# An S5 and an H3 layer in one kernel: the same operations under another written-out order

## The chip, the core and the metric

The kernel runs on one NeuronCore of a Trainium2 chip. The metric is the device time of one execution in microseconds. PE is TensorE, DVE is VectorE, ACT is ScalarE, POOL is GpSimd and SP is SyncE; SP does no arithmetic here and only issues DMAs.

## What is computed

Two sequence layers over 2048 tokens and 640 channels, their outputs side by side in one 2048 x 1280 result.

```python
# A (S5): a complex diagonal recurrence between two projections
Lam_bar = exp(dt * Lam);  B_bar = ((Lam_bar - 1) / Lam)[:, None] * Bmat
Bu = einsum("bld,pd->blp", x, B_bar)
for t in range(L):
    h = Lam_bar * h + Bu[:, t]            # hs collects h
y = 2 * einsum("blp,dp->bld", hs, Cmat).real + x * Dskip
# B (H3): a four-tap shift convolution, then a long convolution over the sequence
k_shift = sum(k_pad[:, t:t + S] * shift_k[:, ks - 1 - t] for t in range(4))
kv = k_shift * v
y = irfft(rfft(kv, 2 S) * rfft(ssm_k, 2 S))[:S] + kv * ssm_D
out_B = q * y
```

## The kernel before

**A program and an order.** `build` lists 779 operations, each with the engines that may run it, the stretch of memory that it reads and writes, and, where it uses PSUM, a group that takes one or two of PSUM's eight banks. `depend` derives from the footprints which operation must follow which. `emit` then walks through `ORDER`, a string with one word for each operation, and issues them in that order; each engine works through its own words strictly in turn. A word is the operation's number, the engine that runs it and its first bank:

```python
order = [(int(x[:-2]), x[-2].upper(), int(x[-1])) for x in ORDER.split()] ...
c.P.narrow = {int(x[:-2]) for x in ORDER.split() if x[-2] == "t"}
```

A stands for ACT, V for DVE, G for POOL, T or t for PE (t: a first Fourier step in its narrow form), S for SP. An operation that opens a group waits until the last one that held its banks is done:

```python
if o is o.group.ops[0]:
    need |= {held[b] for b in own if held[b] is not None}
```

All tiles lie in one SBUF tile, `arena`, at fixed places, and PSUM is one tile, `acc`; so the profile names nearly every operand `arena` or `acc`, and lines tell the operations apart.

**Part A.** `load_x` brings x in eight transposed pieces (x0 to x7), `load_B` the input matrix (two parts by a transposing DMA, B2, the rest by way of PE, `turn_B`). The recurrence is a tree over 16 neighbouring steps. `up2` (ten of them, L558; pieces x4 to x7), `up1` (five, L558 and L579; x2 and x3) and `up0a` to `up0c` (x0 and x1) multiply by B and combine pairs of steps with the matrices RR; `coarse` scans over the blocks of 16 (`cs_...`, mostly DVE); `down` spreads the result over the steps again. A `down` sum is added by DVE (L701), or, where ACT evicts it (L699), PE first adds the old value through an identity matmul (L681) for each matmul of its own (L682). `project` is C0 to C15, each 20 matmuls (L718): it loads 128 rows of x (`ld_r`, L709), multiplies them by Dskip (`xd`, L710), adds them to the product (`ev_C`, L720) and stores (`st_A`, L724). Four row buffers turn over, so a load waits for the store four uses before it.

**Tables.** On POOL: integer phases, by `iota` (w_m, g_m: L289, L327) and products (w_q L291, g_q L330, phs L449, phc L452), which wait in part for parameters that a chain of small DVE operations works out; fn1 (L386) is the first on POOL that needs them. ACT makes sines of them (w_s, g_s L334, sin, cos, al_s). DVE makes the RR from them (al, then `rr`, L436).

**Part B.** `load_kv` brings k and v by transposing DMAs (k into a single buffer); `conv` works out kv: four multiplications (`cm`, L199 on ACT, L198 on DVE), three sums (`ca`, L799; the product of each tap goes through one scratch buffer) and the product with v (`cx`, L800). `plane` (`pl`, L806) stores kv to `kv_rows` in HBM and `relay` (`rl`, L816) loads it in another layout. The Fourier transforms are matmuls: `s1` (L835, narrow L840; evicted by `e1`, L845) and `s2` (L859; `e2`, L872) for the filter (h) and for kv (k), in two halves of channels; `product` multiplies the spectra (pp, pq, py, pz: L883 to L890); `r2` (L904; `er2`, L909) and `r1` (L925) go back; `er1` multiplies by q (L937) and `store` writes (`st_B`, L949). `addD` (L768) adds ssm_D to the filter; the first `s1h0` operations need addD0.

**Around the change.** In the first 62 us PE runs up2, up1, up0a and the filter's s1h0 between them; DVE and ACT evict all of them and run conv, POOL builds tables, SP issues the loads one behind the other. Evictions are named `ev_` and the operation.

Of the kernel before, what the change touches and what calls it, by code (L numbers as in the profile page):

```python
# [1040 lines left out]
def plain_order(P):  # L1041
# [16 lines left out]


ORDER = (  # L1060
# [38 lines left out]
)  # L1099


# [68 lines left out]
```

## Time and profile before

| | |
|---|---|
| median of 3 runs (lowest to highest) | 199.89 us (198.49 to 203.23) |
| profiled execution, its own time | 199.76 us |
| its span | 197.9 us |
| mean granted clock of PE | 0.975 |
| instructions | 7928 |
| HBM read / written | 11.32 MB / 7.86 MB |

A row of a timeline is: start and length in us, engine, line and operation, result<-inputs, shapes, and in brackets the idle time of the engine before it with what ended it. A piece of the chain is: start, length, what. A row of the stage view is: the stretch, its length, then busy us (and instructions) of PE, PE's weight loads, DVE, ACT and POOL, the granted clock, the busy share of the DMA engines and GB/s. A row of a group is: line, engine, operation, shapes and count, then busy us, mean ns of one, idle us before them.

### The profile page before, as it was taken

The page shows a single profiled execution, that of the slowest core. Times are in us where ns is not written, and L with a number is a line of the kernel's source. Part 1 is how long each engine was busy: PE and PEld are TensorE (multiplying, and loading weights), DVE is VectorE, ACT ScalarE, POOL GpSimd, SP SyncE. Part 2 cuts the span into 40 slices and gives each one's busy share as a digit, 9 for nine tenths or more (in the row PEclk, how much of TensorE's full clock was granted, in tenths as well). Part 3 has the DMA queues.
Part 4 walks back from the last instruction along what each step waited for, and adds up shares of the span by engine and source line. Part 5 has one row for each costly group of instructions (what it writes and reads, how often), then busy time and mean ns, then how long its engine had stood idle before and what let it go on. Part 6 is the DMA issues. An engine that isn't in the chain of part 4 may idle for free.

```text
span 197.9 us, 7928 instructions
## 1 busy us (share of the span) xinstructions
PE 178.1 (90%) x3546; PEld 119.9 (61%) x3549; DVE 173.3 (88%) x230; ACT 134.0 (68%) x160; POOL 76.5 (39%) x63
## 2 busy tenths in 40 slices
PE   5699999779999999788978999999999999999970
PEld 1386555345567765556656666567677867887750
DVE  3969998999789899999999999999999999858650
ACT  2076999845998798999969799796377640870000
POOL 6869972940020400341704465840220604605000
PEclk9799999969999999999999999999999999999996
DMA  6999999599599999899993899002599805433995
GB/s 140 224 206 160 170 170 146 125 183 176 121 231 213 174 179 124 134 193 137 149 251 80 223 165 192 8 3 68 114 211 213 168 14 155 111 85 83 233 208 160
DMA packets 106685, 30.19 MB, mean 153 GB/s; under 512 B 101275, under 2 KB 106011, under 8 KB 106651
## 3 DMA queue, kind: packets, MB, share of 16 engines
q1 hardware_dynamic: 106158, 29.18, 81.0%
q8 instruction: 28, 0.46, 1.1%
q10 hardware_dynamic: 492, 0.50, 1.0%
q14 instruction: 7, 0.05, 0.1%
HBM read 11.32 MB, written 7.86 MB: 97 GB/s over the span
## 4 chain that ended last, share of the span: by engine, by line
PE 41%; DVE 20%; POOL 16%; DMA 9%; issue 7%; ACT 5%; DVEq 0%; ACTq 0%; POOLq 0%
PE acc L718 17%; PE acc L558 8%; POOL arena L291 5%; POOL arena L799 4%; PE acc L904 4%; ACT arena L872 4%; PE acc L859 3%; DMA arena<-in_B_ssm_D_dram 3%; PE acc L840 3%; POOL arena L330 3%; PE acc L925 2%; DMA kv_rows<-arena 2%; DMA arena<-in_A_Lambda_re_dram 2%; DVE arena L872 2%; DVE arena L198 2%
## 5 line engine op out<-in xcount | busy, mean ns | idle before, releaser
L558 PE MATMUL acc<-arena 128*64 128x512 bf16 (+1 forms) x440 | 46.8, 369 | 0.1
L718 PE MATMUL acc<-arena 128*128 128x320 bf16 x320 | 45.7, 300 | 0.6 <-DVE arena L720 0.4
L872 ACT CAST arena<-acc 128x960 bf16<-128x960 f32 (+1 forms) x38 | 33.3, 910 | 9.2 <-PE acc L859 7.4
L718 PEld LDWEIGHTS <-arena 128*128 128x128 bf16 x320 | 30.4, 98 | 13.3 <-DVE arena L720 1.0
L558 PEld LDWEIGHTS <-arena 128*64 128x64 bf16 x440 | 24.6, 113 | 18.7 <-issue 2.4
L845 ACT CAST arena<-acc 128x1024 bf16<-128x1024 f32 x32 | 31.1, 1024 | 7.0 <-PE acc L840 6.6
L909 ACT CAST arena<-acc 128x1024 bf16<-128x1024 f32 x18 | 17.4, 1026 | 9.9 <-PE acc L904 9.8
L859 PE MATMUL acc<-arena 128*64 128x160 bf16 x512 | 21.8, 235 | 1.4 <-ACT arena L845 0.4
L859 PEld LDWEIGHTS <-arena 128*64 128x64 bf16 x512 | 18.1, 110 | 6.4 <-ACT arena L872 1.7
L710 POOL TENSOR_TENSOR arena<-arena 128x640 bf16<-128x640 bf16 x9 | 12.3, 1399 | 15.9 <-DVE arena L888 9.3
L799 DVE TENSOR_TENSOR arena<-arena 128x2048 bf16<-128x2048 bf16 x13 | 18.2, 1401 | 0.3
L720 DVE TENSOR_TENSOR arena<-acc,arena 128x640 bf16<-128x640 f32 x16 | 13.1, 823 | 5.8 <-PE acc L718 4.8
L799 POOL TENSOR_TENSOR arena<-arena 128x2048 bf16<-128x2048 bf16 x2 | 8.3, 4154 | 22.5 <-DVE arena L198 22.5
L886 POOL TENSOR_TENSOR arena<-arena 128x1280 bf16<-128x1280 bf16 x4 | 10.6, 2656 | 16.2 <-DVE arena L883 10.7
L701 DVE TENSOR_TENSOR arena<-acc,arena 128x1024 bf16<-128x1024 f32 (+1 forms) x14 | 16.1, 1169 | 0.3 <-PE acc L682 0.2
L888 POOL TENSOR_TENSOR arena<-arena 128x1280 bf16<-128x1280 bf16 x3 | 8.3, 2772 | 20.0 <-DVE arena L886 19.9
L840 PE MATMUL acc<-arena 64*64 64x64 bf16 x960 | 11.8, 195 | 4.4 <-POOL arena L330 2.5
L840 PEld LDWEIGHTS <-arena 64*64 64x64 bf16 x960 | 9.6, 108 | 9.9 <-issue 4.1
L937 DVE TENSOR_TENSOR arena<-acc,arena 128x960 bf16<-128x960 f32 (+1 forms) x12 | 12.1, 1041 | 2.1 <-PE acc L925 2.1
L198 DVE TENSOR_SCALAR arena<-arena 128x2048 bf16<-128x2048 bf16 (+2 forms) x19 | 12.6, 674 | 1.1 <-issue 0.5
L682 PE MATMUL acc<-arena 128*128 128x512 bf16 (+2 forms) x50 | 12.3, 328 | 0.5 <-ACT arena L845 0.5
L883 DVE TENSOR_TENSOR arena<-arena 128x2560 bf16<-128x2560 bf16 x8 | 12.0, 1504 | 0.2
(142 smaller groups left out, 289.3 us busy)
## 6 DMA issues: line engine op xcount, KB each, us to landing
out_dram<-arena SPq DMA_DIRECT2D x32, 160.0 KB, 3.5
arena<-in_B_ssm_k_dram SPq DMA_DIRECT2D x8, 320.0 KB, 6.4
kv_rows<-arena SPq DMA_DIRECT2D x5, 512.0 KB, 3.5
arena<-kv_rows SPq DMA_DIRECT2D x16, 160.0 KB, 4.4
arena<-in_A_x_dram SPq DMA_DIRECT2D x16, 160.0 KB, 3.6
arena<-in_B_q_dram SPq DMA_DIRECT2D x8, 320.0 KB, 5.7
arena<-in_A_B_im_dram ACTq DMA_DIRECT2D x2, 160.0 KB, 4.1
arena<-in_A_B_re_dram ACTq DMA_DIRECT2D x1, 160.0 KB
```

The lines of the kernel that those rows point to most:

```text
L198: vm = lambda e: lambda out, in_, by: e.tensor_scalar_mul(out=out, in0=in_, scalar1=by)
L558: e.matmul(o[64 * r:64 * r + 64], lhsT=self.BT[j][:, r, d, :], rhs=self.XP[:, d, lo:lo + n], start=(d == 0), stop=(d == 4), skip_group_che ...
L682: e.matmul(B[:, o], lhsT=c.RR[:, n, j, :], rhs=fr(j, q, k), start=not by_pe, stop=True, skip_group_check=True)
L701: e.tensor_tensor(out=o, in0=b, in1=o, op=ALU.add)
L718: e.matmul(B[:, 512 * b:512 * b + 320], lhsT=lh[j], rhs=self.CT[:, j, 320 * b:320 * b + 320], start=(j == 0), stop=(j == 9))
L720: P.add(f"ev_C{i}", {PDVE: dve(640)}, lambda e, B: e.tensor_tensor(out=ys.rearrange("p (b n) -> p b n", b=2), in0=B.rearrange("p (b n) -> ...
L799: P.add(f"ca{d}_{j}", tt, lambda e: e.tensor_tensor(out=t1, in0=t1, in1=t2, op=ALU.add), outs=[t1], ins=[t1, t2])
L840: e.matmul(B[64 * b:64 * b + 64, 512 * l + 64 * i:512 * l + 64 * i + 64], lhsT=lh[i][ps], rhs=F[ps, b, 64 * l:64 * l + 64], start=True, st ...
L845: P.add(f"e1{what}{hf}_{u}", {PACT: act(1024), PDVE: dve(1024)}, lambda e, B: c.CP[e](out=out, in_=(B.rearrange("p (l n s k) -> p k s l n" ...
L859: e.matmul(B[64 * s:64 * s + 64, 512 * b + 160 * i:512 * b + 160 * i + 160], lhsT=c.W[:, k, 64 * b:64 * b + 64], rhs=self.AS[hf][:, k, 160 ...
L872: c.CP[e](out=out, in_=b.rearrange("p r (k j n) -> p r k j n", k=n, j=4) if nj > 1 else b.rearrange("p r (k x) -> p r k x", k=n))
L909: P.add(f"er2{hf}_{u}", {PACT: act(1024), PDVE: dve(1024)}, lambda e, B: c.CP[e](out=out, in_=B.rearrange("p (s n b) -> p b s n", s=2, n=4 ...
```

## The change

`ORDER` alone is replaced. It has the same 779 words' numbers; 53 of them name another engine or queue: 38 evictions, convolution taps and small copies change between DVE and ACT (19 each way), seven go from DVE to POOL (xd0, xd1, xd7, xd10, xd12, py0, pz1) and five from POOL to DVE (k0, one pq0, xd4, one py1, xd11), and three small loads change between ACT and SP. Among the `down` sums, ad0_2 and ad1_6 go to ACT and ad0_9 to DVE. The narrow forms are the same ones. Banks differ in many places. The head and the tail of the string:

```diff
 ORDER = (
-    "152A0 50G0 140S0 109V0 0V0 75V0 145G0 98G0 6T0 26G0 141G0 153A0 77S0 38G0 146S0 147A0 41G0 168S0 78A0 22G0 13G0 8G0 14V0 "
-    "59G0 4T1 76A0 159S0 15V0 19V0 7G0 18V0 57V0 9V0 112V0 16V0 23V0 111V0 58V0 17V0 28V0 3T0 60G0 148T1 35V0 24V0 167S0 71G0 "
...
-    "698S0 680V4 771T0 686S0 687S0 685S0 697S0 688S0 761T4 772V0 767V2 760V0 768S0 696S0 773S0 762V4 763S0"
+    "146A0 26G0 152S0 0V0 41G0 75V0 5T0 76A0 77S0 98G0 7G0 147A0 167S0 135G0 50G0 71G0 153A0 6T1 78S0 8G0 59G0 158S0 9V0 99G0 "
+    "67G0 1T0 13G0 15V0 16V0 14V0 19V0 17V0 18V0 51V0 168S0 53V0 150T1 57V0 33V0 58V0 28V0 68G0 80T0 4T2 81V0 82A0 140S0 156T0 "
...
+    "771T2 767V4 768S0 770G0 698S0 696S0 695S0 760G0 761T4 697S0 772V2 688S0 687S0 773S0 778S0 762V4 763S0"
 )
```

The stretches that matter, read engine by engine (names for numbers, the bank behind a colon):

```text
PE, up2 to the first s1h0
- up21_0 21_2 21_2 21_0 21_4 21_6 21_8  up20_2 20_0 20_8 20_4 20_6  up1_0:6 up1_4:2 s1h0_0:6 s1h0_7:0 up1_8:4 ...
+ up21_0 21_2 21_0 21_4 21_8 21_6 21_2  up20_8 20_0 20_6 20_4 20_2:4  up1_0:0 s1h0_1:4 s1h0_7:2 up1_4:6 up1_6:2 ...
POOL, from the first operation that needs parameters to the table gm
- fn1 off fn fn fn s16 ph g_m phs w_q w_q w_m w_m g_q w_q phc addD0 w_q g_q g_q r16 gm      (one g_q ahead of fn1)
+ fn1 w_m g_m w_q sw phs fn fn c30 fn g_q g_q dm0 ph w_q w_m w_m w_q w_q g_q addD0 phc r16 gm (one g_q ahead of fn1)
DVE, ahead of the first s1h0
- ev_up21_0 f1 rr rr na ev_up20_2 ca0_2 cm0_1 ca0_1 ma rr cm0_0 rr ev_up20_6 ev_up1_0 ca0_0 e1h0_7
+ cm0_2 ev_up21_4 ca0_2 ev_up21_6 ev_up20_8 al f1 rr rr ca0_1 cm0_0 ev_up20_6 ev_up20_2 ev_up1_0 e1h0_7 ca0_0 rr
ACT, the same stretch
- f1_s al_s ev_up21_2 cm0_3 i_s ev_up21_6 g_s cm0_2 g_s ev_up21_4 w_s w_s ev_up20_0 ev_up20_8 ...
+ ev_up21_0 cm0_3 ev_up21_8 f1_s cm0_1 g_s g_s al_s i_s ev_up21_2 w_s ev_up20_0 sin ev_up20_4 ...
SP, the first loads
- ld_sk par Braw0 x7 B2 x6 B2 k0 x4 x5 x3 h0 h0 x2 h0 h0 D v0 k1 v1 x0 D x1 C0 k2 C0 pl0 v2 pl1 ...
+ Braw1 par x6 par B2 x7 sk B2 k0 x4 x5 h0 h0 x2 h0 x3 D h0 v0 k1 C0 v1 x0 x1 pl0 Dr k2 v2 C0 pl1 ...
DVE, from cs_v0 to cx4 (some left out)
- e2h0_12 e2h0_30 cs_v0_m cx2 cs_a0 cm3_2 cs_w0 cs_s0 ... cx3 ev_gC3_0 ev_gC0_0 cm4_3 cm4_2 e2k0_0 ... addD1 pp0 xd0 ev_C0 e1h1_6 e2k0_8 cx4
+ e2h0_9 cx2 cs_v0_m cs_a0 cs_w0 cs_s0 cm3_3 ... cx3 cm4_3 cm4_2 ad1_0 e2k0_0 ... addD1 pp0 ev_C0 e1h1_6 e2k0_8 e1h1_2 cx4
SP, the stores and loads around cx4
- v4 r1 r3 pl3 rl1 pl4 q1 st_A0 rl1 ...
+ v4 st_A0 rl1 pl3 pl4 rl1 ...
SP, the tail
- st_A10 r9 r11 r8 r14 st_B0 st_A11 r15 st_A9 r13 st_B0 st_A8 5x st_B0 st_A15 r12 st_B1 st_B0 st_B1 st_B1 st_B1 st_B1 st_B1 st_B1 st_A13 st_B1 st_A14 st_A12
+ r11 st_B0 st_A11 r15 st_A9 st_A8 st_B0 st_B0 st_A10 st_B0 r13 4x st_B0 r14 st_B1 r12 st_B1 st_A13 6x st_B1 st_A14 st_A15 st_A12
PE, the tail (both)
  C8, three r11, C15, three r11 (their order differs), C13, C14, C12
```

70 rows, old and new, of the table ORDER are left out of this document.

## The prediction

> **What bounds the kernel now.** The page comes first: its busy line, its slices and the chain that ended last.
>
> ```profile
> PE 178.1 (90%) x3546; PEld 119.9 (61%) x3549; DVE 173.3 (88%) x230; ACT 134.0 (68%) x160; POOL 76.5 (39%) x63
> PE   5699999779999999788978999999999999999970
> PEclk9799999969999999999999999999999999999996
> PE 41%; DVE 20%; POOL 16%; DMA 9%; issue 7%; ACT 5%; DVEq 0%; ACTq 0%; POOLq 0%
> ```
>
> The reader is to see an engine that is hardly ever free: PE is busy 178.1 of 197.9 us and holds 41% of the chain, and DVE is nearly as full. An order can win only where PE's digit is below 9: in the first three slices, in slices 8 and 9 (35 to 45 us), in some of 17 to 22, and in the tail. The chain of waits in order of time names those places.
>
> ```profile
> 40.78 0.76 PE acc L840 x64
> 41.54 3.86 PE acc L558 x20
> ...
> 59.35 2.28 PE acc L558 x20
> 61.63 0.46 PE acc L579 x8
> ...
> 108.07 4.51 DMA kv_rows<-arena
> ...
> 191.93 0.82 DVE arena L720
> ```
>
> The same twenty matmuls of L558 take 3.86 us at 41.54 and 2.28 us at 59.35. The stage view and the timeline of PE show why.
>
> ```profile
> 40.00:50.00 10.00, 9.22 (x214) 4.99 (x216) 9.82 (x12) 5.59 (x5) 2.02 (x2) 0.83 0.89 171
> 90.00:100.00 10.00, 9.55 (x168) 6.50 (x159) 9.49 (x12) 9.97 (x14) 4.06 (x1) 1.00 1.20 135
> 130.00:140.00 10.00, 9.96 (x196) 7.17 (x182) 9.52 (x11) 7.74 (x9) 1.11 (x1) 1.00 0.12 37
> ```
> ```profile
> 10.98 7.22 PE L558 MATMUL acc<-arena 128*64 128x256 bf16 x102
> 40.78 0.41 PE L840 MATMUL acc<-arena 64*64 64x64 bf16 x27 [2.51 <-POOL arena L330]
> ```
>
> PE idles 2.51 us ahead of 40.78, and in 40 to 50 us the granted clock is 0.83 where the other two stages have 1.00. One stall, paid twice: 2.51 idle and 3.86 - 2.28 = 1.6 at a slow clock, 4.1 us in all. From 120 us on PE works through (9.96 of 10.00 in 130 to 140), so the order cannot win there.
>
> The profile puts that idle down to a POOL product of L330. I read it otherwise: the waiting instruction is the first of s1h0_0, whose result goes to bank 6, and bank 6 is freed by ev_up1_0 on DVE, whose row below ends at 40.68.
>
> ```profile
> 18.34 3.17 DVE L436 TENSOR_TENSOR arena<-arena 128x1280 bf16<-128x1280 bf16 x1
> 21.43 3.18 DVE L436 TENSOR_TENSOR arena<-arena 128x1280 bf16<-128x1280 bf16 x1
> 31.64 1.22 DVE L799 TENSOR_TENSOR arena<-arena 128x2048 bf16<-128x2048 bf16 x1
> 32.86 1.48 DVE L436 TENSOR_TENSOR arena<-arena 128x1280 bf16<-128x1280 bf16 x1
> 39.47 1.21 DVE L599 CAST arena<-acc 128x1024 bf16<-128x1024 f32 x1
> ```
> ```profile
> 11.43 0.19 POOL L386 COPY arena<-arena 128x10 int32<-128x10 int32 x1 [1.71 <-DVE arena L378]
> 16.23 3.93 POOL L291 TENSOR_TENSOR arena<-arena 128x1024 int32<-128x1024 int32 x2
> 23.22 3.14 POOL L291 TENSOR_TENSOR arena<-arena 128x1024 int32<-128x1024 int32 x1
> 33.58 1.20 POOL L768 TENSOR_TENSOR arena<-arena 128x80 bf16<-128x80 bf16 x1 [4.94 <-DMA arena<-in_B_ssm_D_dram]
> ```
>
> DVE is late because it takes turns with POOL. The spread rr (L436) lasts 1.48 us at 32.86, when POOL rests, and 3.17 at 18.34, when POOL is in the two products of 16.23 that end at 20.16: 20.16 + 1.4 is its end. In return the product of 23.22 takes 3.14 instead of 3.93 / 2 = 1.96, for DVE's second rr runs until 24.61. So an operation of DVE with both inputs in the arena and a product of POOL exclude each other.
>
> **The change part by part.** No instruction is added or removed but one: two of the `down` sums (ad0_2, ad1_6) go from DVE to ACT and one (ad0_9) comes back. The rest is order, banks, 53 operations on other engines or queues, and the queue of SP.
>
> **1. The first stage, to the end of up0a_0 (before: 61.63 + 0.46 = 62.1).** POOL's products are packed differently: after fn1 (11.43, which I leave there, since the chain of small DVE operations ahead of it is as long) come all four w_q and three g_q, phs and ph, and only then addD0; phc follows. Unblocked that is 7 x 1.96, 2.3 for phs and some 4 of small ones, 20 us: 31.8. ACT decides when DVE can go on:
>
> ```profile
> 17.19 2.00 ACT L199 ACTIVATE arena<-arena 128x2048 bf16<-128x2048 bf16 x1 [1.40 <-DMA arena<-in_B_k_dram]
> 21.09 1.15 ACT L334 ACTIVATE arena<-arena 128x1024 bf16<-128x1024 int32 x1
> ```
>
> cm0_3 ends at 19.2 again (same load of k); ca0_2 on DVE must let a g_q finish and ends near 22; ACT's cm0_1 writes the buffer that ca0_2 reads, 22 to 24; two g_s of 1.15 follow, then al_s at 26.2. From there DVE and POOL alternate: al, f1 to 27.0; rr 1.4; w_q 1.85; rr 1.4; w_q 1.85; ca0_1 1.15; g_q 1.85; cm0_0 0.75: 37.2. addD0 ends at 38.4, and DVE's next two, ev_up20_6 and ev_up20_2 (1.21 each, as the row of 39.47), at 39.5. On PE, s1h0_1 stands right behind up1_0 and writes bank 4, which ev_up20_2 frees. PE begins up2 at about 11.3 (10.98 before; x7 is issued after x6 and half of B2), needs 2.28 x 24 / 20 = 2.7 for an up1, and for the ten up2 what it needed before (it ran from 10.98 to 40.78 - 2.51 with ten up2 and two up1, so 27.3 - 5.4 = 21.9): up1_0 ends at 35.9. So it waits some 3.6 us, the old stall moved forward, with one up1 less done ahead of it.
>
> Then, to the end of up0a_0: before 62.1 - 40.8 = 21.3 with 1.6 of slow clock in it; after 39.5 + 19.7 + 2.7 for up1_4 = 61.9 at full clock, 63.5 if the clock drops. Against 62.1 that is -0.2 or +1.4; without knowing which, **+0.6**. The ends: no wait at all gives 35.9 + 22.4 = 58.3, -3.8; +4.1 on top is rival B. Cover: PE is fed to 35.9 by up2 and up1_0, and nothing hides the rest.
>
> [...]
>
> **2. From up0c to pl4 (62 to 112).** DVE sets the pace (9.49 of 10.00 in 90 to 100, and the chain runs through it to pl4's transfer at 108.07). Its rows by kind:
>
> ```profile
> L845 DVE CAST arena<-acc 128x1024 bf16<-128x1024 f32 x8 | 9.7, 1220 | 1.4 <-PE acc L840 1.4
> L710 DVE TENSOR_TENSOR arena<-arena 128x640 bf16<-128x640 bf16 x7 | 3.4, 482 | 0.0
> L552 DVE CAST arena<-acc 128x640 bf16<-128x640 f32 x3 | 2.4, 809 | 0.0
> L681 PE MATMUL acc<-arena 128*128 128x512 bf16 x8 | 3.1, 383 | 0.1
> ```
>
> Between cs_v0_m and cx4 DVE loses ev_gC0_0 (0.81, now ACT), cx2 (1.22, as the row of L799; now ahead of cs_v0_m, where DVE waits for PE anyway) and xd0 (0.48, now on POOL, which was free there), and gains e1h1_2 (1.22, ahead of cx4). PE does 0.4 more of s2h0 ahead of cs_v0. Sum -0.81 - 1.22 - 0.48 + 1.22 + 0.4 = **-0.9**. If ACT (9.97 of 10.00 in 90 to 100) is late with ev_gC0_0, 0.8 of it goes. The wait added on SP, st_A0 for ev_C0 ahead of pl3 and pl4, holds pl3 back to about 105; pl4 cannot go before cx4 anyway, so it costs 0 to 0.6, and I take 0.
>
> **3. 112 to the last C.** PE's own work decides. ACT evictions of `down` make PE add the old value through an identity: two more by ACT, one fewer, each of two 512-wide matmuls at some 0.22 start to start (L681's 383 ns overlap): 2 x 0.22 = **+0.4**. The moves of pq0, py0, py1, pz1 between DVE and POOL have slack: r20 and r21 are behind a C of 2.8 us each.
>
> **4. The tail.**
>
> ```profile
> 179.25 0.33 SPq L724 DMA_DIRECT2D out_dram<-arena  x1
> ...
> 185.88 5.73 SPq L949 DMA_DIRECT2D out_dram<-arena  x8
> ...
> 193.52 1.53 SPq L724 DMA_DIRECT2D out_dram<-arena  x2
> ```
>
> From st_A8 (179.25) to the last store SP issues 20 DMAs almost without a pause, to 195.05; its last two go out from 193.52, when ev_C12 has been done since 192.75 (191.93 + 0.82), so SP itself is late there. In the new queue 24 stand at st_A8 or behind it: ld_r13, ld_r14, st_A10 and one st_B0 more. At the cheapest price, 0.33, four cost 1.3; at the mean of 15.8 / 20 = 0.79 they cost 3.2; under waits, nothing. I take **+0.7**. It also brings ld_r12 closer to xd12 and ev_C12; by the rows that still just fits.
>
> **The sum.** The profiled execution lasted 199.76: 197.9 of span and 1.9 around it. 199.76 + 0.6 - 0.9 + 0.4 + 0.7 = 200.6. The median shown, 199.89, is 0.1 above that execution, so nothing is shifted.
>
> **The rivals.**
> **A, the early stall goes.** If POOL and DVE collide less than I chain them, PE runs on at 35.9: -3.8, and no slow clock. Half of the gain of part 2 is lost with it, DVE being the next bound: 199.76 - 3.8 - 0.5 + 0.4 + 0.7 = 196.6. For it: DVE has one rr and one ev less ahead of the critical eviction. Against: every two-input row beside POOL took the long time.
> **B, slower: x1 arrives late.** SP puts half of C0 (3.99 us of issue) ahead of v1, x0 and x1, and k1 must wait for cm0_0.
>
> ```profile
> 43.35 3.99 SPq L533 DMA_TRANSPOSE arena<-in_A_C_im_dram  x1
> ```
> ```profile
> arena<-in_A_x_dram SPq DMA_TRANSPOSE x8, 5.3
> ```
>
> k1 goes out at 37.3 (behind cm0_0, 37.2); k1 and v1 at 2 each, C0 at 4 and the two x at 1.5 each end their issue at 48.3; x1 lands 5.3 later, 53.6, and up0a_4 comes on PE at 53 to 54.7. It decides as soon as x1 is over 2.5 us behind PE: 2.5 of idle and 1.6 of clock, 200.6 + 4.1 = 204.7. For it: DMA is near full there (0.89). Against: no landing of that stage held PE before.
> **C, nothing moves.** The bound after 120 us is PE's work, the same but for 0.4, and early gains or losses are taken up by DVE: 199.76 + 0.4 = 200.2.
> **D, SP in the tail.** The four issues at 0.79, 3.2 instead of 0.7: 200.6 + 2.5 = 203.1.
>
> **How the numbers follow.** Forecast 0.38, A 0.20, B 0.10, C 0.20, D 0.12. A measurement here tells about 2% (4 us) from no change. Range 196.6 to 203.6: A's point, and D with part of B; it leaves out A's lower half and most of B. Over 2% faster (below 195.9) needs A with part 2 whole: 0.13. Over 2% slower (above 203.9): B and a little of D, 0.12. Within: 0.75. Predicted time 200.6.
>
> **What would show it.** Part 1: PE idle ahead of s1h0_1 between 36 and 39.5 and rr at 2.5 us or more; no idle there, or granted clock 1.00 in 30 to 50, speaks for A. B: PE waiting at L558 for in_A_x. Part 2: kv_rows' last store about 0.4 us sooner than 108.07. Part 3: twelve instead of eight 512-wide identity matmuls. Part 4: SP without a pause from st_A8 on, and more than the 6.0 us of before from the end of C12 (191.9) to the end of the span (197.9). My chain in part 1 would be wrong if POOL's and DVE's operations did not alternate one by one.

## The result and the profile after

The changed kernel is slower: median 207.1 us of four executions (204.66 to 209.35) against 199.38 of the kernel before on the same chip, ratio 1.0365 (95%: 1.0265 to 1.0465). The profiled execution took 204.66, with a span of 202.9. The median is understood only with the spread: of ten executions, these four and six more below, three took 204.6 and seven 207.1 to 209.7, and the ratio leaves the slowest out.

The page of the changed kernel, its busy line, slices and chain:

```profile
PE 179.4 (88%) x3548; PEld 121.0 (60%) x3551; DVE 170.6 (84%) x228; ACT 131.0 (65%) x160; POOL 79.2 (39%) x65
PE   5399979899999989889979999999899799899850
PEclk9769999999999999999999999999999999999995
DMA  6999999799999999799977999460786102206986
PE 43%; DVE 23%; POOL 11%; DMA 7%; SPq 5%; issue 5%; ACT 1%; POOLq 1%; DVEq 0%
```

PE is busy 1.3 us longer than before and stands 3.7 longer. The low clock of slices 8 and 9 is gone; instead the low stretch in the head, slices 2 and 3, has grown from 3.4 to 6.8 us. In slices 32 to 36 the DMA engines rest at zero to two tenths, right ahead of the stores at the end, and SP's own queue holds 5% of the chain. The waits of PE, by what ended them (line, releaser, us in total, times, longest):

```profile
PE acc L356 <- DMA arena<-in_A_log_dt_dram: 2.5, 1, 2.5
...
PE acc L904 <- DVE arena L872: 1.2, 1, 1.2
PE acc L558 <- DVE arena L575: 1.0, 1, 1.0
...
PE acc L840 <- POOL arena L452: 1.0, 1, 1.0
...
PE acc L718 <- DVE arena L720: 0.9, 1, 0.9
```

These are new: the head (log_dt's load), r20_8 at 159.6 (L904), up20_0 at 28.0 (L558), s1h0_1 at 40.6 (L840) and C12 at 192.6 (L718). Operation by operation, after against before:

| ends at, us | before | after |
|---|---|---|
| begin of the first up2 | 10.98 | 13.43 |
| up0a_0 | 62.07 | 62.89 |
| cs_s0 | 72.69 | 72.62 |
| cs_h1 | 87.34 | 89.35 |
| cx4 | 108.04 | 109.58 |
| C7 | 154.25 | 154.55 |
| C8 | 178.26 | 180.84 |
| C12 | 191.89 | 195.51 |
| span | 197.9 | 202.9 |

Of the 1.5 us at cx4 only 0.3 are left at C7. Then 2.3 are lost between C7 and C8, 1.0 more up to C12, and 1.4 behind it. (Some 0.6 is only moved from ahead of C7 to behind it, with r20_9, which now follows C7.) The tail, first SP's queue of the changed kernel, then DVE's:

```profile
172.75 0.34 SPq L709 DMA_DIRECT2D arena<-in_A_x_dram  x1
173.14 8.98 SPq L724 DMA_DIRECT2D out_dram<-arena  x2
182.17 2.27 SPq L949 DMA_DIRECT2D out_dram<-arena  x2
...
185.59 0.53 SPq L709 DMA_DIRECT2D arena<-in_A_x_dram  x1
...
193.38 4.42 SPq L949 DMA_DIRECT2D out_dram<-arena  x6
197.90 2.05 SPq L724 DMA_DIRECT2D out_dram<-arena  x3
```
```profile
191.73 0.82 DVE L720 TENSOR_TENSOR arena<-acc,arena 128x640 bf16<-128x640 f32 x1 [3.08 <-POOL arena L710]
195.43 0.82 DVE L720 TENSOR_TENSOR arena<-acc,arena 128x640 bf16<-128x640 f32 x1 [2.87 <-POOL arena L710]
196.78 0.82 DVE L720 TENSOR_TENSOR arena<-acc,arena 128x640 bf16<-128x640 f32 x1 [0.52 <-POOL arena L710]
```

The row of 8.98 us is two stores: st_A9, and st_A8, which stands at the queue's head from 173.6 until ev_C8 lets it go at 181.8. Behind it wait stores and loads that could have gone: in e1 below the loads of r13 and r14 go out at 177.57 and 179.25. Here r13 is issued at 185.59 and lands at 190.17; xd13 on POOL and ev_C13 (191.73) follow, so PE waits 0.87 ahead of C12 for the bank that ev_C13 frees; r14 goes the same way, and ev_C12 runs at 196.78 although C12 ended at 195.51.

### The profile page after: what moved, and what is told of

Read it like the earlier page. It is cut to its first block, busy times and chain, and to the rows that moved or that the text cites. A ratio compares the mean times of both kernels' runs of the same rounds, so it can differ in the third digit from the quotient of the medians.

```text
span 202.9 us, 7950 instructions
## 1 busy us (share of the span) xinstructions
PE 179.4 (88%) x3548; PEld 121.0 (60%) x3551; DVE 170.6 (84%) x228; ACT 131.0 (65%) x160; POOL 79.2 (39%) x65
## 4 chain that ended last, share of the span: by engine, by line
PE 43%; DVE 23%; POOL 11%; DMA 7%; SPq 5%; issue 5%; ACT 1%; POOLq 1%; DVEq 0%
PE acc L718 11%; PE acc L558 8%; PE acc L904 6%; PE acc L859 6%; DVE arena L701 4%; POOL arena L291 4%; PE acc L579 3%; PE acc L840 3%; SPq L949 3%; DMA arena<-in_B_ssm_k_dram 3%; DVE arena L720 2%; PE acc L682 2%; DMA arena<-in_A_x_dram 2%; DVE arena L845 2%; DMA arena<-in_A_log_dt_dram 2%
## 5 line engine op out<-in xcount | busy, mean ns | idle before, releaser
L558 PE MATMUL acc<-arena 128*64 128x512 bf16 (+1 forms) x440 | 45.8, 363 | 1.3 <-DVE arena L575 1.0
L718 PE MATMUL acc<-arena 128*128 128x320 bf16 x320 | 45.9, 299 | 1.1 <-DVE arena L720 0.9
L718 PEld LDWEIGHTS <-arena 128*128 128x128 bf16 x320 | 30.4, 98 | 13.8 <-DVE arena L720 1.2
L558 PEld LDWEIGHTS <-arena 128*64 128x64 bf16 x440 | 24.9, 111 | 19.2 <-DVE arena L575 1.5
L845 ACT CAST arena<-acc 128x1024 bf16<-128x1024 f32 x33 | 32.0, 1021 | 4.2 <-PE acc L840 3.3
L710 POOL TENSOR_TENSOR arena<-arena 128x640 bf16<-128x640 bf16 x12 | 17.6, 1473 | 36.5 <-DMA arena<-in_A_x_dram 36.5
L859 PE MATMUL acc<-arena 128*64 128x160 bf16 x512 | 22.6, 235 | 2.6 <-DVE arena L720 1.0
L909 ACT CAST arena<-acc 128x1024 bf16<-128x1024 f32 x16 | 15.5, 1023 | 12.3 <-PE acc L904 10.8
L859 PEld LDWEIGHTS <-arena 128*64 128x64 bf16 x512 | 18.1, 110 | 8.7 <-ACT arena L872 1.9
L198 DVE TENSOR_SCALAR arena<-arena 128x2048 bf16<-128x2048 bf16 (+2 forms) x19 | 14.4, 771 | 4.9 <-DMA arena<-in_B_k_dram 4.4
L799 DVE TENSOR_TENSOR arena<-arena 128x2048 bf16<-128x2048 bf16 x13 | 16.9, 1301 | 0.4
L701 DVE TENSOR_TENSOR arena<-acc,arena 128x1024 bf16<-128x1024 f32 (+1 forms) x13 | 14.9, 1165 | 0.4 <-PE acc L682 0.4
L840 PEld LDWEIGHTS <-arena 64*64 64x64 bf16 x960 | 9.7, 108 | 7.0 <-issue 1.9
L904 PE MATMUL acc<-arena 64*128 64x128 bf16 x320 | 12.1, 226 | 1.6 <-DVE arena L872 1.2
L840 PE MATMUL acc<-arena 64*64 64x64 bf16 x960 | 11.7, 195 | 1.7 <-POOL arena L452 1.0
L886 POOL TENSOR_TENSOR arena<-arena 128x1280 bf16<-128x1280 bf16 x3 | 8.0, 2673 | 12.2 <-DVE arena L883 12.2
L904 PEld LDWEIGHTS <-arena 64*128 64x128 bf16 x320 | 10.9, 145 | 2.9 <-DVE arena L872 1.3
```

The lines of the kernel that those rows point to most:

```text
L558: e.matmul(o[64 * r:64 * r + 64], lhsT=self.BT[j][:, r, d, :], rhs=self.XP[:, d, lo:lo + n], start=(d == 0), stop=(d == 4), skip_group_che ...
L701: e.tensor_tensor(out=o, in0=b, in1=o, op=ALU.add)
L710: P.add(f"xd{i}", {PDVE: dve(640, .52), PPOOL: 1.5}, lambda e: e.tensor_tensor(out=ys, in0=ys, in1=c.DR, op=ALU.mult), outs=[ys], ins=[ys, ...
L718: e.matmul(B[:, 512 * b:512 * b + 320], lhsT=lh[j], rhs=self.CT[:, j, 320 * b:320 * b + 320], start=(j == 0), stop=(j == 9))
L799: P.add(f"ca{d}_{j}", tt, lambda e: e.tensor_tensor(out=t1, in0=t1, in1=t2, op=ALU.add), outs=[t1], ins=[t1, t2])
L840: e.matmul(B[64 * b:64 * b + 64, 512 * l + 64 * i:512 * l + 64 * i + 64], lhsT=lh[i][ps], rhs=F[ps, b, 64 * l:64 * l + 64], start=True, st ...
```

## Experiments

Orders are shown per engine, in extracts; each run changes nothing but the words shown. Each ratio is to the kernel before, run beside it on the same chip.

**SP's tail, taken out of the changed kernel (e1) and put into the kernel before (e8).**

```diff
 SP, changed kernel (e1)
-st_A9 st_A8 st_B0 st_B0 st_A10 st_B0 ld_r13 4x st_B0 ld_r14
+st_A9 st_B0 st_B0 st_A10 ld_r13 ld_r14 st_A8 5x st_B0
 SP, kernel before (e8); POOL: xd14 behind xd13
-ld_r14 st_B0 st_A11 ld_r15 st_A9 ld_r13 st_B0 st_A8 st_B0
+st_B0 st_A11 ld_r15 st_A9 st_A8 st_B0 st_B0 ld_r13 ld_r14
```

> The changed kernel; alone in SP's queue st_A8 goes behind two st_B0, st_A10, ld_r13 and ld_r14, which were ready while SP stood at st_A8 (173.6 to 181.8 us, DMA at 0 to 2 tenths). Theory (the queue's order in the tail is half of the loss): POOL's xd13 no longer waits for ld_r13 until 190.2, C12 no longer waits 0.87 for ev_C13, ev_C12 follows C12 at once; end of C12 to end of span back from 7.4 to about 6.0, span 2.2 to 2.6 shorter than 202.9. Rival (the tail is bound by what DMA can carry or SP can issue, the order is no matter): span within 0.5 of 202.9.

> The kernel before with one part of the change alone, SP's tail: st_A8 with two st_B0 ahead of the loads of r13 and r14 (xd14 moved behind xd13 on POOL, as it must be then). Theory: SP stands at st_A8 until ev_C8 (179.2), r13 is issued at about 180.5 and r14 behind it, ev_C13 and ev_C14 move back behind xd13 and xd14 on POOL, and PE waits ahead of C12: 0.5 to 2.5 us slower than before, about 200.5 to 201.5. Rival: in this order POOL and DVE have room for it, and the loads still land in time: 199.4, same as before within 0.4.

e1: 205.97 median, profiled 203.38; ratio to before 1.0275 (1.0144 to 1.0406). From C8's end to the end of the span: 22.06 in the changed kernel, 20.64 here, 19.64 before. e8: 201.59 against 199.89, ratio 1.0114 (1.0069 to 1.0158); C12 ended as before (192.03 against 191.89), but ev_C12 1.6 later. DVE in e1, and POOL in e8:

```profile
189.26 0.82 DVE L720 TENSOR_TENSOR arena<-acc,arena 128x640 bf16<-128x640 f32 x1 [0.48 <-PE acc L718]
191.98 0.82 DVE L720 TENSOR_TENSOR arena<-acc,arena 128x640 bf16<-128x640 f32 x1 [1.89 <-PE acc L718]
194.70 0.82 DVE L720 TENSOR_TENSOR arena<-acc,arena 128x640 bf16<-128x640 f32 x1 [1.89 <-PE acc L718]
```
```profile
186.14 1.40 POOL L710 TENSOR_TENSOR arena<-arena 128x640 bf16<-128x640 bf16 x1 [8.36 <-DVE arena L937]
187.89 1.40 POOL L710 TENSOR_TENSOR arena<-arena 128x640 bf16<-128x640 bf16 x1 [0.34 <-DMA arena<-in_A_x_dram]
```

In e1 the last three ev_C wait for PE and no longer for POOL, and PE no longer waits ahead of C12. The gain from C8's end is 1.4 in the profiled execution, less than the 2.2 to 2.6 expected, and from C12's end it is still 7.0 us to the end of the span, not 6.0. The median of e1 does not show it: its ratio and the changed kernel's overlap. Put into the kernel before, the tail costs 1.7 in the median, and the ratio's interval leaves out 1. So the cost is measured in e8, and the way it comes about is seen in the rows of both. In e8 C12 did not wait; the loss came behind it, so "PE waits ahead of C12" missed. The 1.0 that e1 leaves against before goes with SP's backlog: st_A12 goes out 3.8 behind C12's end, before 2.3.

**The head (e2), head and tail (e3).**

```diff
 SP
-Braw1 par x6 par B2 x7 sk B2
+Braw1 par par x7 B2 x6 sk B2
```

> The changed kernel; alone in SP's queue the load of log_dt and x7 go ahead of x6 (the first eight words: Braw1, two par, x7, B2, x6, sk, B2). Theory: t_par comes at about 7.5 instead of 8.8 and the first up2 at about 11.2 instead of 13.4, but the eviction ev_up20_2 on DVE that frees the bank of s1h0_1 comes only 0 to 1 us sooner, since k's load and the turns of DVE and POOL decide it: PE's idle ahead of s1h0_1 grows from 1.0 to 2 to 3 us, up0a_0 ends 0 to 1 sooner, the span gets 0 to 1 shorter. Rival (PE's late start passes through to the end): span 2.2 shorter or more.

> The changed kernel with both edits of SP's queue, tail and head. Theory: tail 2.2 to 2.6 and head 0 to 1 add up: span 199.5 to 200.7, still 1.5 to 3 over the kernel before, for PE's waits in the middle (1.2 us ahead of r20_8 and others). Rival (head passes through): span 198 or less, the kernel before reached. Rival (tail bound by DMA): 202 or more.

e2: 206.29, ratio 1.031 (1.0161 to 1.0459). The first up2 began at 11.30 instead of 13.43, up0a_0 ended 0.8 sooner, as expected, and C8 ended at 181.10 instead of 180.84: absorbed. The wait ahead of s1h0_1 was 1.15, not the 2 to 3 expected. e3: 206.86, from 202.14 to 209.64, so the sum of both gains did not come; the range holds e1's median and e2's, and no order among the three is shown. The profile is of the highest execution, and it showed the first two of the variable places: cm0_0 at 36.28 took 2.69 instead of 0.95, and DVE's wait for the third k transpose was 2.92 instead of 0.88, after which PE stood 3.99 ahead of a filter step (L859) at 71.3.

**The stall of the kernel before (e4), and a try to beat both (e12).**

```diff
 DVE, kernel before (e4; e12 has both)
-... cm0_0 rr ev_up20_6 ev_up1_0 ca0_0
+... cm0_0 ev_up20_6 ev_up1_0 rr ca0_0
 (e12)
-cs_a0 cm3_2 cs_w0 cs_s0
+cs_a0 cs_w0 cs_s0 cm3_2
```

> The kernel before; alone on DVE the fourth rr (3.17 us at 35.24, in turns with POOL) goes behind ev_up1_0. Theory (bank 6 and ev_up1_0 hold s1h0_0, not POOL's g_q): ev_up1_0 ends near 38, PE's idle of 2.51 ahead of s1h0_0 and the slow clock behind it go, up0a_0 ends at 58 to 59.5 instead of 62.1; DVE, the next bound, gives part of it back, span 1 to 3.5 shorter. Rival (the profile's releaser: POOL's L330, ending at 40.2): the idle stays, span within 0.5.

> The kernel before with the fourth rr behind ev_up1_0, as in the experiment that took away its stall at 38 us, and with cs_w0 and cs_s0 on DVE ahead of cm3_2 (which waits for the fourth k transpose). Theory: the 1.8 us won at up0a_0 were lost again because DVE stands at cm3_2 from 68.5 to 69.4 and runs it ahead of cs_s0; now cs_s0 ends near 70.5, 1.5 sooner, and the kernel comes to 197.3 to 198.3, 0.5 to 1% faster than before. Rival (the load of r6 pins C7 at 151.3): cs_s0 ends sooner, but C7 still starts at 151.3 and the time is 198.8.

PE in the kernel before, then in e4:

```profile
40.78 0.76 PE L840 MATMUL acc<-arena 64*64 64x64 bf16 x64 [2.51 <-POOL arena L330]
41.47 3.93 PE L558 MATMUL acc<-arena 128*64 128x512 bf16 x20
```
```profile
38.20 0.71 PE L840 MATMUL acc<-arena 64*64 64x64 bf16 x64
38.84 2.35 PE L558 MATMUL acc<-arena 128*64 128x512 bf16 x20
```

POOL's order is the same in both, yet the wait and the low clock are gone. POOL's product that the row names ran like this in e4:

```profile
37.05 1.89 POOL L330 TENSOR_TENSOR arena<-arena 128x1024 int32<-128x1024 int32 x1
```

It ended at 38.94, 0.7 behind the begin of s1h0_0. So the bank held by DVE was the releaser, as the prediction read it, and not POOL's product. Of the 4.1 us that it cost, 2.3 come back as a wait ahead of up1_6 at 44.3; the 1.8 left at up0a_0 shrink to 0.6 at cs_s0 and to 0 at C7, and the median is 198.85 against 199.35, ratio 1.0006 (0.9954 to 1.0058). e12 brought cs_s0 to 70.34 (before 72.69), C7 to 152.45 (154.25) and the span of its profile to 196.4 (197.9), so the r6 load does not pin C7; but its median is 199.22 against 199.29, ratio 1.0013 (0.9974 to 1.0052), with executions up to 204.5, and not the 197.3 to 198.3 expected. No version that measurably beats the kernel before was found.

**Where the upper executions come from.** The changed kernel again (a0), and two edits meant for the third k transpose (e5, e7).

```diff
 DVE, e5 and e7
-ca0_0 rr cx0 na cm1_3 cm1_2 ca1_2 den rr den cm1_1 ca1_1 cm1_0
+ca0_0 cx0 cm1_3 cm1_2 ca1_2 cm1_1 ca1_1 cm1_0 rr den rr den na
 e7 alone (and SP's tail as in e1)
-pz1 pz1 e2k1_24
+e2k1_24 pz1 pz1
```

> The changed kernel itself once more, to see how its executions spread. Theory: its order has so little slack where DVE waits for the third k transpose (0.88 us in the profile taken) that the time falls on two levels, about 204 and about 207 to 209 us, and the median is near 206.5; a profile that falls on the upper level shows a DVE wait of 2.5 us or more for in_B_k ahead of cm2 at about 59 us, and cs_v0 on PE 3 us or more later than 68.45. Rival: the executions scatter evenly because every transfer varies a little; then the profile shows no single wait grown and the lateness builds up over many stages.

> The changed kernel with two range reductions (rr), two steps of den and one of na moved on DVE from the stretch at 44 to 51 us to just behind cm1_0, whose end lets the third k transpose be issued. Theory: cm1_0 ends 3 us sooner (about 50), the load is issued and lands 3 us sooner, DVE's wait of 0.88 us at 58.4 goes, and the upper level goes with it: median 204 to 205, no execution above 206.5. Rival (the levels come from elsewhere): the wait goes, but executions of 207 and more stay and the median stays near 206.5.

> Three edits on the changed kernel at once: SP's tail as in the first experiment (st_A8 behind two st_B0, st_A10 and the loads of r13 and r14), the third k transpose sooner as in the experiment beside this one, and e2k1_24 ahead of the two pz1 on DVE, so that r20_8 on PE does not wait (1.21 us at 159.55). Theory: 1.4 from the tail, 1.0 to 1.2 from r20_8, and the upper level gone: median 201 to 202.5. Rival (PE's lateness is made up elsewhere and lost again at the next wait): only the tail's 1.4 shows, 203 to 205.

a0: 207.27 (204.55 to 209.73), profiled 207.13. cm2_3 ran at 59.28 (59.33 in the first profile), so the theory of the k transpose failed for this execution. Its span is 2.3 longer. At cx4 it is 0.2 behind the first profile and at C6's end 0.8 (150.23 against 149.40), in small pieces, as the rival had it; one wait adds 1.0 at 151, in the rows of DVE and PE:

```profile
151.37 0.49 DVE L710 TENSOR_TENSOR arena<-arena 128x640 bf16<-128x640 bf16 x1 [0.91 <-DMA arena<-in_A_x_dram]
```
```profile
152.84 0.71 PE L904 MATMUL acc<-arena 64*128 64x128 bf16 x16 [0.98 <-DVE arena L720]
```

xd6 waits for r6's load, ev_C6 follows, r20_7 waits for the bank that ev_C6 frees, and C7 comes 1.8 later. r6's load stands behind st_A2, whose ev_C2 DVE runs 2.8 after C2's end.

e5 failed outright: 208.69, all six between 207.65 and 209.7, ratio 1.0468 (1.0428 to 1.0507). The cause lies ahead of the edit. DVE and POOL, in the changed kernel's faster profile:

```profile
37.26 0.95 DVE L198 TENSOR_SCALAR arena<-arena 128x2048 bf16<-128x2048 bf16 x1
38.13 2.34 DVE L575 CAST arena<-acc 128x1024 bf16<-128x1024 f32 x2
```
```profile
36.67 0.98 POOL L768 TENSOR_TENSOR arena<-arena 128x80 bf16<-128x80 bf16 x1 [4.25 <-DMA arena<-in_B_ssm_k_dram]
37.43 2.95 POOL L452 TENSOR_TENSOR arena<-arena 128x1280 int32<-128x1280 int32 x1
```

and in e5, with PE:

```profile
37.48 2.69 DVE L198 TENSOR_SCALAR arena<-arena 128x2048 bf16<-128x2048 bf16 x1
40.09 2.34 DVE L575 CAST arena<-acc 128x1024 bf16<-128x1024 f32 x2
```
```profile
35.81 0.73 POOL L768 TENSOR_TENSOR arena<-arena 128x80 bf16<-128x80 bf16 x1 [3.18 <-DMA arena<-in_B_ssm_k_dram]
36.30 3.31 POOL L452 TENSOR_TENSOR arena<-arena 128x1280 int32<-128x1280 int32 x1
```
```profile
42.53 0.70 PE L840 MATMUL acc<-arena 64*64 64x64 bf16 x64 [2.74 <-issue]
43.17 4.03 PE L558 MATMUL acc<-arena 128*64 128x512 bf16 x20
```

The load that addD0 waits for let it start 0.9 sooner. So phc (L452) had started when cm0_0 (L198) came: 2.69 instead of 0.95. The two evictions behind cm0_0 end 2.0 later, PE stands 2.74 instead of 1.0, and the next twenty matmuls take 4.03 instead of 2.35: 3.6 us at up0a_0 (66.51 against 62.89), from a load that came early. In these rows the one of the two that comes second is drawn out: in the changed kernel cm0_0, 0.17 ahead of phc, takes 0.95 and phc 2.95 (in e13, with no such neighbour, 2.32); in e5 cm0_0, 1.18 behind phc, takes 2.69 and ends 0.6 behind phc's end. Why all six executions of e5 lie high was not settled.

e7: 205.68, ten executions from 200.59 to 210.4. The wait at r20_8 is gone (C7's end to C10's begin 4.2 instead of 5.6), and the fastest execution is 4 us below the changed kernel's; the spread stays. cm1_0 ended 3.2 sooner, as meant, but DVE still waited 1.27 for the third k transpose (0.88 in the changed kernel), which took 4.24 of issue instead of 3.21.

**Evictions first (e9), with the later places (e10), with the head (e11).**

```diff
 DVE, e9 to e11
-ca0_1 cm0_0 ev_up20_6 ev_up20_2 js1 ev_up1_0
+ev_up20_6 ev_up20_2 ca0_1 cm0_0 js1 ev_up1_0
 e10, e11 also: DVE (e2k1_24 as in e7, SP's tail as in e1; e11: the head as in e2)
-pp1 pq1 ad0_8 ev_C2
+pp1 ev_C2 pq1 ad0_8
```

> The changed kernel with one exchange on DVE: the evictions ev_up20_6 and ev_up20_2 ahead of ca0_1 and cm0_0 instead of behind them. Theory: which of cm0_0 (DVE) and phc (POOL) starts first at 37 us decides an execution: cm0_0 first takes 0.95, phc first makes it 2.69, ev_up20_2 ends 1.7 later, PE stands 2.74 instead of 1.0 ahead of s1h0_1 and the clock is halved for 3.4 us, 3.4 in all. With the evictions ahead of both, s1h0_1 follows up1_0 at once (39.6) in every execution: the upper level loses 3 to 4 us, the median falls from 207.2 to 203.5 to 205, and none lies above 207.5. Rival (the levels come from the later places, the load of r6 at 149 and the third k transpose at 59): the gap at 40 goes, but the median stays at 206 to 207.

> The changed kernel with four places mended at once: the two evictions first as in the experiment beside this one; ev_C2 on DVE directly behind the first pp1 of its stretch, so that st_A2 and the load of r6 go 2 us sooner; e2k1_24 ahead of the two pz1; SP's tail as in the first experiment. Theory: 1.4 from the tail, 1.2 from r20_8, 0.5 to 1.0 from r20_7 and the upper level at 40 us gone: median 200 to 202, within 1% of the kernel before. Rival (more places of the new order bind, each hidden behind the one before): 203 or more.

> The same four places and SP's head as in the second experiment (log_dt's load and x7's transpose sooner). Theory: with the wait for ev_up20_2 gone the head's 2.1 us are no longer absorbed at 40 us; at least 1 us of them is left at up0a_0's end, and the median is 0.5 to 1.5 below the kernel beside this one. Rival (DVE sets the first stage, not PE): up0a_0 ends within 0.5 of the kernel beside it and the medians agree.

210.34, 208.51 and 207.22; ratios 1.0587 (1.0541 to 1.0634), 1.0495 and 1.0411. All three forecasts failed. In e9 the gap at 40 is gone (s1h0_1 at 39.72), and PE has this instead; below it SP's queue in e9, then in the changed kernel:

```profile
57.89 4.48 PE L558 MATMUL acc<-arena 128*64 128x512 bf16 x20 [3.82 <-DMA arena<-in_A_x_dram]
```
```profile
41.58 1.87 SPq L773 DMA_TRANSPOSE arena<-in_B_k_dram  x1
43.55 3.18 SPq L533 DMA_TRANSPOSE arena<-in_A_C_im_dram  x1
46.77 3.72 SPq L773 DMA_TRANSPOSE arena<-in_B_v_dram  x1
50.54 3.40 SPq L524 DMA_TRANSPOSE arena<-in_A_x_dram  x2
```
```profile
38.23 2.02 SPq L773 DMA_TRANSPOSE arena<-in_B_k_dram  x1
40.35 2.99 SPq L533 DMA_TRANSPOSE arena<-in_A_C_im_dram  x1
43.40 3.20 SPq L773 DMA_TRANSPOSE arena<-in_B_v_dram  x1
46.65 3.73 SPq L524 DMA_TRANSPOSE arena<-in_A_x_dram  x2
```

This is the way of rival B. k1 waits on SP for cm0_0, and C0, v1, x0 and x1 stand behind it. With cm0_0 3.3 later, x1 is 3.9 later, PE stands 3.82 and the clock is halved for 6.8 us: 6.4 at up0a_0. In the changed kernel's profile x1 was in time by less than that.

**cm0_0 itself moved (e13), with the later places (e14), with the head (e15).**

```diff
 DVE, all three (e14 and e15 also the places of e10; e15 also the head)
-al dc f1 dc rr rr dc ca0_1 cm0_0 ev_up20_6
+ca0_1 cm0_0 al dc f1 dc rr rr dc ev_up20_6
```

> The changed kernel with ca0_1 and cm0_0 on DVE moved into the 1.35 us that DVE waits ahead of al at 29.9, away from phc on POOL. Theory: cm0_0 ends at 32 to 33 instead of 38.2 in every execution, so the second k transpose leaves SP at 35.8 instead of 38.2 and x0 and x1 2 us sooner (x1 is in time with room); ev_up20_2 ends about 1 us sooner (39.3), the PE wait of 1.0 ahead of s1h0_1 nearly goes, and an execution can no longer lose the 3.4 us of phc before cm0_0: median 203.5 to 205 and the highest below 207.5. Rival (the upper executions come from the r6 load at 149 and the third k transpose alone): up0a_0 ends sooner, the median stays at 206 to 207.

> The same with three later places of the new order mended: ev_C2 directly behind the first pp1 of its stretch, e2k1_24 ahead of the two pz1, and SP's tail with st_A8 behind two st_B0, st_A10 and the loads of r13 and r14. Theory: these three are worth 0.5 to 1, 1.2 and 1.4 where nothing ahead of them is late; median 200 to 202, within 1.5% of the kernel before. Rival: 203 or more, since each place hides another.

> The same four places and the head (log_dt's load and x7's transpose sooner). Theory: 2.1 us sooner at the first up2; with the wait at 40 us gone, 0.5 to 1.5 of it is left at the end, 199.5 to 201.5, so that the five places together account for the whole loss against the kernel before. Rival (DVE sets the first stage): equal to the kernel beside it within 0.5.

| | median (lowest to highest) | ratio to before |
|---|---|---|
| a0, changed kernel | 207.27 (204.55 to 209.73) | 1.0327 (1.0258 to 1.0397) |
| e13 | 204.99 (203.65 to 207.22) | 1.0302 (1.0263 to 1.0340) |
| e14 | 202.89 (201.09 to 204.22) | 1.0201 (1.0150 to 1.0252) |
| e15 | 202.68 (201.09 to 204.37) | 1.0194 (1.0131 to 1.0258) |

DVE and POOL in e13:

```profile
31.28 2.27 DVE L198 TENSOR_SCALAR arena<-arena 128x2048 bf16<-128x2048 bf16 x1
```
```profile
37.27 2.32 POOL L452 TENSOR_TENSOR arena<-arena 128x1280 int32<-128x1280 int32 x1
```

cm0_0 still meets a POOL product, but in a stretch where DVE had to wait, and phc runs its 2.32 undisturbed here. (In e14 and e15 phc meets an rr instead and takes 3.6, and PE waits 1.29 ahead of s1h0_1.) The median falls by 2.3, or by 1.5 against the kernel before (199.89 beside a0, 199.12 beside e13), the fastest execution by 0.9, and the ratio hardly moves. Five of six executions lie at or below 205.12, where three of ten did. So it is likely that the upper executions are what went, but six executions do not show it. Whether the collision or x1 behind it made each of them this does not separate, since both go with cm0_0.

The later places give 2.1 more, of 3.1 to 3.6 expected. Where the rest stays is seen in the rows of PE and DVE in e15:

```profile
163.76 5.61 PE L718 MATMUL acc<-arena 128*128 128x320 bf16 x40 [1.09 <-DVE arena L720]
```
```profile
162.88 0.82 DVE L720 TENSOR_TENSOR arena<-acc,arena 128x640 bf16<-128x640 f32 x1
```

C11 waits for the bank that ev_C10 frees. In all five runs that move e2k1_24 (e7, e10, e11, e14, e15) the 1.21 ahead of r20_8 is gone, and 1.06 to 1.09 stand ahead of C11 instead. From C7's end to the end of the later of C9 and C11 these five take 15.1 us, the changed kernel 15.35, the kernel before 13.6. So that move is worth 0.3 and not 1.2. DVE sets this stretch: from ev_C7's begin to ev_C10's end it takes 9.1 in the changed kernel, 9.0 in e15, 7.9 before. In the same way the move of ev_C2 took away xd6's wait for r6, but in all four runs that have it r20_7 waits 0.7 for ev_C6.

The head gives 0.2 in the median, which is nothing. up0a_0 ends 0.5 sooner than in e14 for a start 2.0 sooner; in e13, whose order up to there is that of e14, it ended at 61.95, sooner than in both. As the rival had it, PE's start does not set the first stage.

e15's median is still 3.6 of the 7.4 to 7.7 us above the kernel before. In its profile (201.31, span 199.4) 1.5 are left. It has C7's end of before (154.29 against 154.25) and the old 6.0 from C12's end to the end of the span; C12 ends 1.5 later, and nearly all of that comes up between C7 and C11, as above: the wait ahead of C11, and some 0.6 for r20_9, which stood ahead of C7 before. An order that takes this stretch back was not run. The other 2 us of the median, spread between executions, stay open.

## Why the prediction was wrong

The forecast was 200.6 with 203.6 as the upper end; it was 207.1. By the stretches of the profile (to up0a_0, to cx4, to C8, behind it) the four parts were to be +0.6, -0.9, +0.4 and +0.7, and measured +0.8, +0.7, +1.0 and +2.4: 5.0 instead of 0.8. The other 2.4, from the profiled execution to the median, is spread, which the sum put at nothing ("nothing is shifted"). The steps that failed are the price of the tail, the slack that part 3 leaned on, the sign of part 2, and that one order has one time.

**What bounds the kernel now.** Right: the bank (e4), the clock (e4), and that DVE and POOL hold each other up (e5: cm0_0 2.69 instead of 0.95). Wrong: "from 120 us on ... the order cannot win there" hid that it can lose there: r20_8 (1.21), r20_7 in a0 (0.98) and C12 (0.87) all lie behind 150.

**Part 1, +0.6.** Measured +0.8, but by another way, and that the two are near is luck. The releaser named, ev_up20_2, was right, and from its end to up0a_0's the sum's 22.4 is what was measured (40.47 to 62.89). The way to it was not. PE did not begin "at about 11.3" but at 13.43, since log_dt's load and x7 stand on SP behind x6; so the wait at s1h0_1 was 1.0 and not 3.6, and the clock held (1.00 in 36 to 50). al began at 31.21 and not at 26.2; half of that is k's load, which left SP at 13.23 (before 10.38), so that cm0_3 did not end "at 19.2 again" but at 21.7. And from al on DVE and POOL did not alternate. POOL's products ahead of addD0 ended at 32.4, then it rested 4.25 for addD0's load, as its row above shows, and both rr ran undisturbed, this one second:

```profile
34.40 1.49 DVE L436 TENSOR_TENSOR arena<-arena 128x1280 bf16<-128x1280 bf16 x1
```

The sign asked for, "rr at 2.5 us or more", failed. The chain began 5.0 late and took 7.0 instead of 11.0 to cm0_0's end, so that "37.2" came out only 1.0 early. What the chain left out is the race at its end, cm0_0 against phc. It is decided within 1 us by a load's landing, and the other outcome costs 3.4 where the clock drops too (e5: 1.7 of idle and 1.7 of slow clock).

**Part 2, -0.9.** Wrong sign: cx4 ended 1.5 later, 0.7 of it beyond the first stage's 0.8. e13, whose first stage ends as before (61.95), shows how. cs_s0 ended 1.1 sooner there, and the sum had 0.8. Then cs_s1 ended as before (81.52; PE came to cs_k0 at 76.27, before at 76.32), and ev_gC3_0 (0.81), not in the sum, stood ahead of cs_h1, which ended 1.0 later. Last, addD1 (L768), before and in e13:

```profile
101.53 0.51 DVE L768 TENSOR_TENSOR arena<-arena 128x80 bf16<-128x80 bf16 x1
```
```profile
101.59 0.52 DVE L768 TENSOR_TENSOR arena<-arena 128x80 bf16<-128x80 bf16 x1 [0.53 <-DMA arena<-in_B_ssm_k_dram]
```

Before, it ran straight behind DVE's own work; in e13 DVE had idled 0.53 for the filter's load. So nothing that DVE had won ahead of it would have counted. The changed kernel waits 0.51 there, to 102.56. Behind addD1 only two of the sum's terms are left, xd0 gone (-0.48) and e1h1_2 come (+1.21): +0.7 where e13 measured 0.6. Adding DVE's instructions over a stretch holds only if no transfer pins it in the middle.

**Part 3, +0.4.** The sum's two more matmuls were right (the sign's "twelve" was a slip; ten, by form):

```profile
L681 PE MATMUL acc<-arena 128*128 128x512 bf16 x10 | 3.8, 383 | 0.0
```

But "PE's own work decides" failed, and with it "r20 and r21 are behind a C of 2.8 us each", the slack that was to cover what happens on DVE. Not the pz1 that went to POOL but two that stayed on DVE (0.81 and 1.92), and now stand ahead of e2k1_24, held r20_8 1.21. The second took 1.92 beside xd10, which the change moved to POOL (156.08 to 157.74), and 0.82 in e7, where xd10 was done (0.82 is also the median of the seven L890 on DVE in the changed kernel). The stretch from C7 to C9 and C11 became 1.7 longer, and e15 shows that DVE sets it.

**Part 4, +0.7.** Measured 2.4 from C8's end, rival D's side of the bounds (up to 3.2). SP's issues were counted; that the queue's head would stand 8 us at st_A8 with loads behind it that could have gone was not (1.4 of it, e1). "By the rows that still just fits" looked at r12; r13 and r14 were late. More than 6.0 from C12's end was right: 7.4.

**The rivals.** A did not come: up1_0 ended at 39.57 and not at 35.9. B did not show in the profiled execution, but its mechanism and its condition, k1 behind cm0_0, are what e9 to e11 ran into; in e9 it cost 6.4, more than the 4.1 put on it, since the clock was halved for 6.8 us. D is most of the tail. The chances treated B and D as apart and took one cost at a time. The tail's 2.4, the missing slack of part 3 and 2.4 of spread came together, and the range held no sum of them.

## What to carry to other kernels

An order written out by hand, or searched with one trace's durations, has to be read for races: wherever two engines that hold each other up (here DVE and POOL, 2.69 instead of 0.95 us for one instruction) meet within a microsecond, price both outcomes and count the worse one. On an in-order queue, look at what stands behind each instruction that waits for another engine, here loads behind a store for 8 us and x1 behind a k buffer's reader. Mending one place of such an order moves the wait to the next: of the 1.21 taken away at r20_8, 1.1 stood ahead of C11 afterwards, and taking one visible stall away (e9) made the kernel 3 us slower, until the operation that tied it to the queue was moved (e13).

## What the runs showed of the hardware

- In the traces of the kernel before and of the changed one the granted clock changed at steps of 3.41 us. It was halved for 3.41 from 7.16 and from 41.29 and again from 194.89 to the end in the kernel before, for 6.83 from 7.29 and again from 198.43 to the end in the changed kernel; the begins lie 10 and 45 steps apart in the one, 56 in the other. The time from PE's stop to the fall of the clock was not fixed. In the kernel before PE idled 2.51 up to 40.78, and the clock fell 3.0 after PE had stopped, 0.5 after it had gone on. In e9 PE idled 3.82 up to 57.89; the clock was 0.75 in 50 to 62 and 0.97 in 62 to 75, which is 6.8 us at half from about 56.0 on, 1.9 after PE had stopped. With the 2.74 idle of e5 the clock was 0.88 in 36 to 50, one stretch of 3.4 at half; with the 1.00 of the changed kernel it was 1.00 there. Why it fell where it did is not shown.
- One DVE instruction on the same tile took 0.95 or 2.69 us by a start 0.2 us ahead of POOL's (changed kernel) or 1.2 behind it (e5).
- The profile named a POOL product as releaser of waits that a PSUM bank held by DVE ended, in the kernel before (e4) and in the changed one: there it names L452, yet in e5 L452 was done at 39.6 and PE went on only at 42.5, behind ev_up20_2 (42.43).
